# k^T v in three bursts instead of five, in a linear-attention and GeGLU block on Trainium2

## The chip, the core and the metric

One core of one Trainium2 chip runs the kernel. The metric is the device time of one execution in microseconds (us). A core has five engines that run side by side, each through its own instructions in order: TensorE (PE, matmuls; its weight loads are listed as PEld), VectorE (DVE), ScalarE (ACT), GpSimd (Pool) and SyncE (SP, which issues the DMAs). They wait for one another through semaphores. A DMA is issued on an engine's queue and lands later.

## The reference, cut to what matters

One sequence of 2048 rows of 640 numbers goes through attention with a feature map instead of a softmax over positions, and then through a GeGLU feed-forward net (1536 wide). There are 32 heads of 20. Shortened:

```python
q, k, v = split(layernorm(x) @ wqkv)             # 32 heads of 20 each
phi_q = [softmax(q @ w_phi), softmax(-(q @ w_phi))]
phi_k = [softmax(k @ w_phi), softmax(-(k @ w_phi))]
kv  = sum over rows of phi_k^T v                 # per head, 40 x 20
z   = sum over rows of phi_k
o   = (phi_q @ kv) / (phi_q . z + 1e-6)
h   = x + o @ wo
out = h + (gelu(layernorm(h) @ w_gate) * (layernorm(h) @ w_up)) @ w_down
```

## The kernel before, in words

**Tiles.** The 2048 rows are 16 tiles of 128. A first stage (up to about 67 us) makes k and v of every tile, and out of them `kv`, the sum over all rows; from then on attention and feed-forward run tile by tile, woven together. The change is in the first stage.

**Weights folded first.** `w_phi` is multiplied into the weights of k and q: `fold` (line 232) makes `Wk2` from the transposed `WkT`, one 128-row piece `d` at a time, into a PSUM tile `wa`, which ACT empties where `d` is in `KA` (line 48, `QA` for q) and DVE elsewhere (lines 256 to 259). The five pieces of k are folded between lines 471 and 482; the five of q at the tiles in `FQ` (line 50), from pieces of `WqT` that `load_T` (line 200) issues on SP as transposing DMAs at the tiles in `LQ` (line 49).

**One tile of the first stage.** The main loop (line 494) does for each tile t: the layer norm of tile t+6 (`ln_ap`, on ACT), which goes to `LN1T` by a transposing DMA on SP; `k_tile` (line 331): ten 128x320 matmuls into `pk` and two exponentials on ACT into `E` (plus and minus); `v_mm` and `v_ev` (lines 301, 315) for tile t+3: ten matmuls into `pv`, evicted by ACT to `vS`, one of `NV` buffers (line 71); and `k_norm` (line 343): DVE sums E over each head (line 347) and takes the reciprocal `rs` (line 351), and two products divide E by it (line 355). Pool does the product of the minus half always and that of the plus half for the tiles in `VP` (line 47); for the others DVE does the plus half, put off into the next tile's `k_norm` (lines 348 and 364), for the last tile at once (line 361).

**k^T v.** `kv_tile` (line 368) adds one tile to `kvp`: 32 matmuls with 32 columns of weights and 40 columns of data each, one per head, four of them side by side in PE's array. They need the tile's two products and its `vS`. The order is written out by hand: `KVG` (line 56) says after which tile's k matmuls which tiles are added (after 6: 0 and 1; after 9: 2 to 4; after 13: 5 to 8); `KVQ` (line 57) puts tiles 9 to 12 behind the first group of q matmuls, and line 539 adds 13 to 15 at the end. Such a run of k^T v matmuls is called a burst. `kv_mask` (line 377) then takes `kvp` through DVE to `KV`, which the first `attn_a` needs.

**q.** `q_mm` (line 387) makes q of one or two column blocks (`QG`, line 52) for 512 rows, 5 or 10 matmuls of 128x512 into `pq`, and `q_exp` (line 399) exponentiates on ACT. Four groups, `QT` (line 53), are done at t=15: groups 0, 1 and 2 of ten matmuls and group 3 of five; the others after `kv_mask` (lines 831 on).

**What sets the order.** Engines follow the program's order. PSUM tiles of this stage (`gtile`, line 111) share four buffers: a tile waits until the one that held its buffer before has been emptied. `kvp` is one of them (line 496).

Of the kernel before, what the change touches and what calls it, by code (L numbers as in the profile page):

```python
# [17 lines left out]
def kernel(  # L18
# [19 lines left out]
    NT = S // P  # L38
    NB = NT // 4
    NC = D // P  # L40
# [3 lines left out]

    H0 = [(P * c) // Dh for c in range(NC)]
    NH = [(P * c + P - 1) // Dh - H0[c] + 1 for c in range(NC)]
    VP = (0, 2, 4, 6, 7, 9, 11, 12)
    KA, QA = (0, 1, 4), (0, 1, 2, 3, 4)
    LQ = (7, 9, 9, 9, 10)
    FQ = (10, 11, 12, 13, 14)  # L50

    QG = ((5, 6), (0, 1), (2, 3), (4,), (7, 8), (9, 10), (11, 12), (13, 14), (15,), (16,), (17,), (18,), (19,))
    QT = (15, 15, 15, 15)
    T3 = 3

    KVG = {6: (0, 1), 9: (2, 3, 4), 13: (5, 6, 7, 8)}
    KVQ = {0: (9, 10, 11, 12)}
    VC = Dh + 1
    KC = Dh + 2

# [7 lines left out]
    SLOT = [(5 * (c // 2) + 2 * (c % 2), 3 * (c // 2) + c % 2, 2 + c % 2) for c in range(NC)]  # L68
    SL = 12
    DC = 512 - 9 * KC  # L70
    NV = 11

    x_v = A_x.rearrange("b (p t) d -> p (b t) d", t=NT)
    o_v = out.rearrange("b (p t) d -> p (b t) d", t=NT)
# [36 lines left out]
    def gtile(name):  # L111
        return psG.tile([P, 2, 512], F32, name=name, tag="G")
# [65 lines left out]

    vF = [p1.tile([P, H * VC + 11], BF16, name=f"vS{i}") for i in range(NV)]
    vS = [v[:, 0:H * VC].rearrange("p (h f) -> p h f", f=VC) for v in vF]  # L180
# [30 lines left out]
    ones = nc.const_aps.tensor(1.0, [P, 512], BF16)  # L211
    for i in range(NV):
        nc.vector.memset(vS[i][:, :, 0], 1.0)
    make_identity(nc, ident)
    nc.gpsimd.memset(hmask, 1.0)
    for c in range(NC):
# [4 lines left out]
                                compare_op=ALU.is_ge, fill=0.0, base=Dh - 1 - off, channel_multiplier=-1)  # L221
    for i in range(NV):
        nc.gpsimd.memset(vF[i][:, H * VC:], 1.0)
# [8 lines left out]
    def fold(WT, W2, quarters, ds=range(NC)):  # L232


        n, w = (2, QF) if quarters else (1, HD)
        runs = []
        for c in range(NC):
            lo, hi = H0[c] * Dh, (H0[c] + NH[c]) * Dh
            for r in range(2 * n):
                a, b = max(lo, r * w), min(hi, (r + 1) * w)  # L240
                if a < b:
                    runs.append((r // n, r, c, a, b))
        runs.sort()
        for d in ds:
            wa = gtile("wa")
            wr = wa.rearrange("p u (q x) -> p (u q) x", q=n)
            for i, (u, r, c, a, b) in enumerate(runs):
                nc.tensor.matmul(wr[:, r, a - r * w:b - r * w], lhsT=WT[:, c, d * P:(d + 1) * P],  # L248
                                 rhs=BD[:, c].rearrange("p a b -> p (a b)")[:, a - H0[c] * Dh:b - H0[c] * Dh],
                                 start=(i == 0 or runs[i - 1][0] != u),  # L250
                                 stop=(i + 1 == len(runs) or runs[i + 1][0] != u), skip_group_check=True)
            dst, src = W2[:, d, :].rearrange("p (u f) -> p u f", u=2), wr[:, :, 0:w]
            if quarters:
                dst = W2[:, d, :].rearrange("p (c r f) -> p r c f", c=NC, r=4)
                src = src.rearrange("p r (c f) -> p r c f", c=NC)
            if d in (QA if quarters else KA):
                nc.scalar.copy(dst, src)
            else:
                nc.vector.tensor_copy(dst, src)
# [19 lines left out]
    def ln_ap(t, on_act=False, on_pe=False):  # L279
        ln = (ln_act if on_act else ln_dve)(p1, "1", *lnp[t])  # L280
        if on_pe:
            lnp[t] = ln
        else:
            transpose_to(LN1T[t // 4][:, :, t % 4 * P:(t % 4 + 1) * P], ln, False)

    def ln_tp(t, on_dve=False):
        transpose_to(LN1T[t // 4][:, :, t % 4 * P:(t % 4 + 1) * P], lnp[t], True, on_dve)
# [13 lines left out]
    def v_mm(t, us=(0, 1)):  # L301
        if 0 in us:
            pv[t] = gtile("pv")
        proj(pv[t], t, Wv, us)
# [10 lines left out]
    def v_ev(t):  # L315
        nc.scalar.activation(vS[t % NV][:, :, 1:VC].rearrange("p (u h) f -> p u h f", u=2),
                             pv[t][:, :, 0:HD].rearrange("p u (h f) -> p u h f", f=Dh), ACTF.Copy,
                             scale=lnp[t][2] if t in CT else 1.0)
# [12 lines left out]
    def k_tile(t):  # L331
        if t in pks:
            pk = pks[t]
            k_part(t, NC - 1)
        else:
            pk = gtile("pk")
            proj(pk, t, Wk2)
        Ek[t] = ev.tile([P, 2, D], BF16, name="E", bufs=10)
        for s in range(2):
            nc.scalar.activation(Ek[t][:, s, :].rearrange("p (u f) -> p u f", u=2), pk[:, :, 0:HD],  # L340
                                 ACTF.Exp, scale=((lnp[t][2], nrstd[t]) if t in CT else (1.0, -1.0))[s])

    def k_norm(t):
# [9 lines left out]
        def mult(s, eng):  # L353
            e = Ek[t][:, s, :].rearrange("p (h f) -> p h f", f=Dh)
            eng.tensor_tensor(e, e, rs[:, s * H:(s + 1) * H, None].to_broadcast([P, H, Dh]), ALU.mult)  # L355

        mult(1, nc.gpsimd)
        if t in VP:
            mult(0, nc.gpsimd)
# [8 lines left out]
    def kv_tile(t):  # L368

        E = Ek[t].rearrange("p s (h f) -> p s h f", f=Dh)  # L370
        for i in range(QH):
            for r in range(4):
                h = r * QH + i
                nc.tensor.matmul(kvp[QUAD[r], :, i * Dh:(i + 1) * Dh], lhsT=vF[t % NV][:, h * VC:h * VC + 32],  # L374
                                 rhs=E[:, :, h, :], start=(i == t == 0), stop=(t == NT - 1), skip_group_check=True)

    def kv_mask():

        for s in range(2):
            dst = bass.AP(KT[s].tensor, KT[s].offset, [KT[s].ap[0], [Dh + 32, QH], [1, Dh]])  # L380
            nc.vector.tensor_scalar(dst, kvp[:, s].rearrange("p (h f) -> p h f", f=Dh), sc[:, s:s + 1], bi[:, s:s + 1],
                                    op0=ALU.mult, op1=ALU.add)
            nc.vector.transpose(KV[s].rearrange("p n j -> p (n j)"), KT[s])
# [3 lines left out]
    def q_mm(j, part=(0, 1), kcs=range(NC)):  # L387

        if 0 in part and 0 in kcs:
            pqs[j] = gtile("pq")  # L390
        for i, bc in enumerate(QG[j]):
            if i not in part:
                continue
            b, c = divmod(bc, NC)
            for kc in kcs:
                nc.tensor.matmul(pqs[j][:, i, :], lhsT=Wq2[:, kc, c * P:(c + 1) * P], rhs=LN1T[b][:, kc, :],  # L396
                                 start=(kc == 0), stop=(kc == NC - 1))

    def q_exp(j, signs=(0, 1)):
        for s in signs:  # L400
            nc.scalar.activation(Eq[j][:, :, s, :], pqs[j][:, 0:len(QG[j])], ACTF.Exp, scale=(1.0, -1.0)[s])  # L401
# [66 lines left out]
    ln_st(4, act=False, between=lambda: ln_ap(3, on_pe=True))  # L468
    ln_tp(3, True)
    nc.sync.dma_start(x_sb[1][:, 2:4, :], x_v[:, 6:8, :])  # L470
    fold(WkT, Wk2, False, (0,))
    v_ev(2)
    fold(WkT, Wk2, False, (1,))
    ln_st(5, act=False, between=lambda: ln_ap(4))
    nc.sync.dma_start(x_sb[2][:, 0:2, :], x_v[:, 8:10, :])
# [18 lines left out]
    for t in range(NT):  # L494
        if t == T3:
            kvp = gtile("kvp")[:, 0, 0:2 * QF].rearrange("p (s f) -> p s f", s=2)
        late = t in (1, 4)
        if 0 < t < NT - 6 and not late:
            ln_ap(t + 6, on_act=True)
        k_tile(t)  # L500
        if t == 0:
            ln_ap(6)
            nc.sync.dma_start(x_sb[3][:, 0:2, :], x_v[:, 12:14, :])
        if t in FQ:
            fold(WqT, Wq2, True, [i for i, f in enumerate(FQ) if f == t])
        for i in KVG.get(t, ()):
            kv_tile(i)
        for j in range(len(QT)):
            if t == QT[j]:
                q_mm(j)  # L510
                q_exp(j)
                for i in KVQ.get(j, ()):
                    kv_tile(i)
        if 0 < t < NT - 3:
            v_mm(t + 3)
        if late:
            ln_ap(t + 6, on_act=True)
        if t == 1:
            nc.sync.dma_start(x_sb[3][:, 2:4, :], x_v[:, 14:16, :])
        if 0 < t < NT - 3:  # L520
            v_ev(t + 3)
        for i in ST.get(t, ()):
            ln_st(i, i + 1)
        k_norm(t)
        load_T(WqT, 0, *[i for i, f in enumerate(LQ) if f == t])
        if t == 10:
            transpose_to(LN1T[0][:, :, P:2 * P], ln_a(1), False)
        if t == 13:
            ln_ap(0, on_act=True)
        if t == 8:  # L530
            for z in KT:
                nc.gpsimd.memset(z, 0.0)
        if t == 13:
            nc.sync.dma_start(Wo, wo_v)
    q = len(QT)
    nc.gpsimd.tensor_copy(Wg[:, 0, 0:1], Eq[q - 2][:, 0, 1, 0:1])
    for a, b in ((0, 2), (2, 4)):
        nc.sync.dma_start(Wg[:, a:b], wg_v[:, a:b])
    for t in range(13, NT):
        kv_tile(t)  # L540
    kv_mask()
    ev_cm.__exit__(None, None, None)
    p1_cm.__exit__(None, None, None)
# [393 lines left out]
```

## Time and profile before

| | us |
|---|---|
| median of three runs | 272.1 (272.08 to 272.21) |
| the profiled execution | 272.0 |
| its span on the core | 270.3 |
| bursts of k^T v, first to last matmul start | 30.7 to 67.0 |
| first matmul of attn_a(0) | 69.1 |

The profile's page comes from one execution. Its views used here: the busy time of each engine; the chain of work that ended last, which is followed back from the last instruction to what released each step; the waits, which say for an idle engine what ended the idle time; and the timeline, where a row has start, length, engine, line, operation, output<-inputs, shapes and count, and in brackets the idle time before it and what ended it. Rows of one kind that follow each other are merged. Starts of matmuls are measured and their ends modelled, so that a difference of starts is the better measure. The granted TensorE clock is 1.00 in every stretch from 15 us on.

### The profile page before, as it was taken

Reading aid. Unit: us, or ns where it says so; the run is one execution under the profiler, and the core shown is the slowest. Engines: PE = TensorE matmul, PEld = TensorE weight load, DVE = VectorE, ACT = ScalarE, POOL = GpSimd, SP = SyncE. Lnnn points to the kernel's source line nnn. Section 1 sums busy time; section 2 is a strip of 40 time slices with the busy share of each in tenths; the row PEclk is TensorE's granted clock in tenths of the full one; section 3 lists DMA queues with packets and bytes.
Section 4 is the critical chain, followed back from the end, with each engine's and each line's share of the span. In section 5 each row is a group of like instructions: output and inputs, shape, how many; then the busy total and the mean of one; then the engine's idle time right before and its main releaser. Section 6 shows DMA issues by size and latency. Waiting matters only on the chain.

```text
span 270.3 us, 7032 instructions
## 1 busy us (share of the span) xinstructions
PE 265.5 (98%) x2851; PEld 171.7 (64%) x2867; DVE 176.4 (65%) x348; ACT 138.1 (51%) x248; POOL 99.5 (37%) x236
## 2 busy tenths in 40 slices
PE   8999999999999999999999999999999999999995
PEld 6777777764455887788755455775555476444574
DVE  5899999998876758876566783568663322333322
ACT  5769997887789675245541356321544300322100
POOL 5448988794002335376211664014561100000000
PEclk9999999999999999999999999999999999999999
DMA  7998255240678432332201224103222101000011
GB/s 192 213 203 175 54 86 100 62 127 26 233 260 232 155 101 62 41 98 51 52 24 51 49 50 51 49 2 78 78 41 52 24 24 51 24 0 0 4 49 49
DMA packets 45264, 22.10 MB, mean 82 GB/s; under 512 B 37808, under 2 KB 43184, under 8 KB 45232
## 3 DMA queue, kind: packets, MB, share of 16 engines
q1 hardware_dynamic: 44576, 21.64, 33.0%
q8 instruction: 22, 0.36, 0.6%
q10 hardware_dynamic: 656, 0.03, 0.2%
q14 instruction: 10, 0.08, 0.1%
HBM read 10.18 MB, written 2.62 MB: 47 GB/s over the span
## 4 chain that ended last, share of the span: by engine, by line
PE 87%; SPq 4%; DVE 2%; POOL 2%; DMA 2%; issue 1%; ACT 1%; ACTq 0%; POOLq 0%
PE gu L767 38%; PE pd L789 20%; PE po L707 8%; PE pq L396 8%; PE pk L296 5%; PE pv L296 4%; SPq L203 2%; PE kvp L374 2%; DMA x_sb<-in_A_x_dram 2%; PE ab L618 1%; POOL E L355 1%; DVE stats L121 1%; PE ab L585 1%; PE wa L248 1%; DVE sk L347 1%
## 5 line engine op out<-in xcount | busy, mean ns | idle before, releaser
L770 ACT ACTIVATE g<-gu 128x512 bf16<-128x512 f32 (+1 forms) x60 | 30.4, 510 | 74.0 <-PE gu L767 73.2
L773 DVE TENSOR_TENSOR GT<-gu,g 128x512 bf16<-128x512 f32 (+1 forms) x60 | 34.4, 580 | 46.6 <-PE gu L767 38.8
L767 PE MATMUL gu<-LN2T,Wg 128*128 128x512 bf16 (+1 forms) x290 | 61.3, 335 | 0.5
L767 PE MATMUL gu<-LN2T,Wu 128*128 128x512 bf16 (+1 forms) x300 | 61.8, 336 | 0.0
L789 PE MATMUL pd<-Wd,GT 128*128 128x320 bf16 (+4 forms) x396 | 53.9, 295 | 0.0
L789 PEld LDWEIGHTS <-GT 128*128 128x128 bf16 x396 | 37.6, 98 | 14.5 <-DVE GT L773 0.2
L767 PEld LDWEIGHTS <-Wu 128*128 128x128 bf16 x300 | 29.4, 98 | 22.6
L767 PEld LDWEIGHTS <-Wg 128*128 128x128 bf16 x300 | 29.0, 98 | 21.2
L296 PEld LDWEIGHTS <-LN1T 128*128 128x128 bf16 x290 | 28.0, 98 | 10.6 <-issue 0.2
L355 POOL TENSOR_TENSOR E<-E,rs 128x640 bf16<-128x640 bf16 x24 | 30.2, 1288 | 6.5 <-DVE rs L351 6.2
L791 DVE TENSOR_TENSOR y<-pd,x_sb 128x320 bf16<-128x320 f32 (+4 forms) x33 | 15.8, 480 | 24.1 <-PE pd L789 24.1
L707 PE MATMUL po<-Wo,oT 128*128 128x320 bf16 x160 | 24.5, 299 | 0.0
L296 PE MATMUL pk<-Wk,LN1T 128*128 128x320 bf16 x160 | 24.4, 299 | 0.0
L396 PE MATMUL pq<-LN1T,Wq 128*128 128x512 bf16 x94 | 22.6, 379 | 0.3
L347 DVE TENSOR_REDUCE sk<-E 128x64 f32<-128x1280 bf16 x16 | 22.9, 1430 | 0.0
L401 ACT ACTIVATE Eq<-pq 128x1024 bf16<-128x1024 f32 (+1 forms) x26 | 19.9, 832 | 2.9 <-PE pq L396 2.7
L707 PEld LDWEIGHTS <-oT 128*128 128x128 bf16 x160 | 15.6, 98 | 7.3 <-ACT oT L165 0.2
L340 ACT ACTIVATE E<-pk 128x640 bf16<-128x640 f32 x28 | 18.7, 746 | 2.7 <-PE pk L296 2.7
L296 PE MATMUL pv<-Wv,LN1T 128*128 128x320 bf16 x130 | 19.8, 299 | 0.1
L151 ACT ACTIVATE ln<-x_sb,v,rstd 128x640 bf16<-128x640 bf16 x14 | 12.9, 920 | 13.0 <-POOL v L746 12.8
L396 PEld LDWEIGHTS <-Wq 128*128 128x128 bf16 x100 | 9.4, 98 | 10.3
L682 DVE TENSOR_TENSOR tt<-AB,w 128x1280 bf16<-128x1280 f32 x10 | 15.1, 1506 | 0.4 <-POOL w L675 0.3
(120 smaller groups left out, 292.3 us busy)
## 6 DMA issues: line engine op xcount, KB each, us to landing
out_dram<-y SPq DMA_DIRECT2D x15, 160.0 KB, 1.8
x_sb<-in_A_x_dram SPq DMA_DIRECT2D x6, 320.0 KB, 3.9
Wu<-in_B_w_up_dram SPq DMA_DIRECT2D x1, 1920.0 KB, 8.8
Wg<-in_B_w_gate_dram SPq DMA_DIRECT2D x2, 768.0 KB, 6.6
Wd<-in_B_w_down_dram SPq DMA_DIRECT2D x1, 1440.0 KB
Wo<-in_A_wo_dram SPq DMA_DIRECT2D x1, 800.0 KB, 5.5
x_sb<-in_A_x_dram SPq DMA_DIRECT2D x4, 160.0 KB, 3.3
Wv<-in_A_wqkv_dram SPq DMA_DIRECT2D x2, 320.0 KB, 4.2
```

Of the source, the lines that this page charges most:

```text
L296: nc.tensor.matmul(ps[:, u, 0:HD], lhsT=lnT(t, c), rhs=W[:, c, u * HD:(u + 1) * HD], start=(c == 0), stop=(c == NC - 1))
L340: nc.scalar.activation(Ek[t][:, s, :].rearrange("p (u f) -> p u f", u=2), pk[:, :, 0:HD], ACTF.Exp, scale=((lnp[t][2], nrstd[t]) if t in C ...
L347: nc.vector.reduce_sum(sk, Ek[t].rearrange("p s (h f) -> p (s h) f", f=Dh), axis=AX.X)
L355: eng.tensor_tensor(e, e, rs[:, s * H:(s + 1) * H, None].to_broadcast([P, H, Dh]), ALU.mult)
L396: nc.tensor.matmul(pqs[j][:, i, :], lhsT=Wq2[:, kc, c * P:(c + 1) * P], rhs=LN1T[b][:, kc, :], start=(kc == 0), stop=(kc == NC - 1))
L401: nc.scalar.activation(Eq[j][:, :, s, :], pqs[j][:, 0:len(QG[j])], ACTF.Exp, scale=(1.0, -1.0)[s])
L707: nc.tensor.matmul(pos[u], lhsT=st[t][:, c, :], rhs=Wo[:, c, u * HD:(u + 1) * HD], start=(c == 0), stop=(c == NC - 1))
L767: nc.tensor.matmul(gu[i][:, 0:n], lhsT=W[:, c, f * P:(f + 1) * P], rhs=LN2T[b][:, c, a0:a1], start=(c == 0), stop=(c == NC - 1))
L770: nc.scalar.activation(g[:, 0:n], gu[0][:, 0:n], ACTF.Gelu_apprx_tanh)
L773: nc.vector.tensor_tensor(st[b, "g", f][:, a0:a1], gu[1][:, 0:n], g[:, 0:n], ALU.mult)
L789: nc.tensor.matmul(pd[:, 0:f1 - f0], lhsT=st[b, "g", f][:, tl * P:(tl + 1) * P], rhs=Wd[:, f, f0:f1], start=(f == 0), stop=(f == NF - 1), ...
L791: nc.vector.tensor_tensor(y[:, f0:f1], pd[:, 0:f1 - f0], x_sb[b][:, tl, f0:f1], ALU.add)
```

## The change

- `KVG` and `KVQ`: k^T v is done in three bursts: tiles 0 to 3 after tile 9's k matmuls, 4 to 8 after tile 13's, and 9 to 15 at the end. The bursts after tile 6 and behind the first q group are gone.
- `NV` is 12 instead of 11: one more buffer of `vS`, with its two memsets.
- The fourth q group (`pq(3)`, five matmuls) is split: two before the last burst, and three, with its exponentials, after it.
- Tile 13 joins `VP`: Pool does both of its products, DVE none.
- `KA` gets piece 3: ACT evicts it and DVE no longer does. `v_ev(2)` comes before fold 0 and not after it.
- `LQ`: W_q's second piece is transposed at tile 8 instead of 9, and so ahead of tile 15's own transpose on SP.

```diff
-    VP = (0, 2, 4, 6, 7, 9, 11, 12)
-    KA, QA = (0, 1, 4), (0, 1, 2, 3, 4)
-    LQ = (7, 9, 9, 9, 10)
+    VP = (0, 2, 4, 6, 7, 9, 11, 12, 13)
+    KA, QA = (0, 1, 3, 4), (0, 1, 2, 3, 4)
+    LQ = (7, 8, 9, 9, 10)
...
-    KVG = {6: (0, 1), 9: (2, 3, 4), 13: (5, 6, 7, 8)}
-    KVQ = {0: (9, 10, 11, 12)}
+    KVG = {9: (0, 1, 2, 3), 13: (4, 5, 6, 7, 8)}
...
-    NV = 11
+    NV = 12
...
+    v_ev(2)
     fold(WkT, Wk2, False, (0,))
-    v_ev(2)
     fold(WkT, Wk2, False, (1,))
...
             if t == QT[j]:
-                q_mm(j)
-                q_exp(j)
-                for i in KVQ.get(j, ()):
-                    kv_tile(i)
+                q_mm(j, kcs=range(2 if j == len(QT) - 1 else NC))
+                if j < len(QT) - 1:
+                    q_exp(j)
...
-    for t in range(13, NT):
+    for t in range(9, NT):
         kv_tile(t)
+    q_mm(q - 1, kcs=range(2, NC))
+    q_exp(q - 1)
     kv_mask()
```

## The prediction

> **What bounds the kernel now.** I read the page's first section, the chain of work that ended last in order of time, and the timeline by engine round each burst of k^T v.
>
> ```profile
> PE 265.5 (98%) x2851; PEld 171.7 (64%) x2867; DVE 176.4 (65%) x348; ACT 138.1 (51%) x248; POOL 99.5 (37%) x236
> ```
>
> TensorE (PE) has work 98% of the time. The chain says from where on that is also what ends last:
>
> ```profile
> 30.84 0.60 ACT E L340
> 31.44 0.04 issue
> 31.48 1.52 PE pv L296 x10
> ...
> 39.79 1.04 PE kvp L374 x96
> ...
> 53.14 1.17 PE kvp L374 x128
> ...
> 59.63 1.16 PE kvp L374 x123
> ...
> 66.29 0.87 PE kvp L374 x96
> ```
>
> Up to 31.44 us the chain runs through the x load at 11.48, VectorE's (DVE's) statistics and ScalarE (ACT); from 31.48 to the last output it is PE, so a microsecond taken out of PE's row there is one off the end, unless something PE waits for is no earlier. A burst is priced by starts, in the timeline:
>
> ```profile
> 29.29 1.52 PE L296 MATMUL pk<-Wk,LN1T 128*128 128x320 bf16 x10
> 30.75 0.68 PE L374 MATMUL kvp<-E,vS 128*32 128x40 bf16 x64
> 31.48 1.52 PE L296 MATMUL pv<-Wv,LN1T 128*128 128x320 bf16 x10
> ```
>
> Ten 128x320 matmuls take 1.36 from start to start, so without its burst pv(9) could begin at 30.65 and not 31.48: 0.83. The same sum gives 1.13 (t=9, 3 tiles), 1.26 (t=13, 4), 1.25 (t=15, 4) and 0.98 (last, 3). Matmuls in a burst start 8.3 ns apart (128: 1.24 less one matmul's 0.187, over 127), 0.264 a tile, and what remains is 0.20 a burst, whatever its size, for the turn from full tiles to 32-column tiles and back. Two bursts cost more than that line: t=6 by 0.10 (pv(9) needs ACT's E(5), which ends at 31.43) and t=9 by 0.14.
>
> **The change, part by part** (times of the trace before).
>
> *Folds.* PE stands before pv(3) because its PSUM buffer is the one ACT empties of fold 0:
>
> ```profile
> 11.62 0.69 ACT L257 CAST Wk<-wa 128x640 bf16<-128x640 f32 x1 [0.66 <-PE wa L248]
> 12.37 1.18 PEld L296 LDWEIGHTS <-LN1T 128*128 128x128 bf16 x9 [0.17 <-issue]
> ```
>
> v_ev(2) now goes first, into ACT's 0.66 of idle time (pv(2) is done at 10.99). By the built program's waits pv(3) then takes the buffer of tile 3's transpose, empty at 11.80: pv(3) at 12.11 for 12.37, 0.25. Of this 0.15 stays: pk(4) (23.86) needs E(2), which ends at 23.67, and ACT there hangs on ln(8) at 21.57, released by Pool's mr behind the x load. Fold 3's eviction, 0.69, fits into ACT's 1.01 idle before 15.64; without that hole it would delay E(0) by 0.69. DVE gets 0.82 free at 14.24 and spends it waiting for the x load until 15.60: nothing. One more pair of memsets (0.14 on DVE, 0.05 on Pool) lies in their idle time before 3.30 and 5.39.
>
> *Burst at t=6 gone*: -0.83. What is late next is ACT, some 2 us behind PE here. In the built program kvp takes its PSUM buffer at its first write, so it now takes it at t=9, and pv(9) waits for v_ev(7) (29.43) and not E(5). Checked one by one up to t=9, PE has 0.4 to 1.0 to spare on each buffer and LN1T landing (nearest: pk(7) at 31.85 against E(5) 31.43).
>
> *t=9 with 4 tiles*: 1.26 for 1.13, +0.13. *t=13 with 5*: +0.26. PE reaches pq(0) at 57.31-0.15-0.83+0.13+0.26 = 56.72.
>
> *W_q's second piece at t=8*: fold 1 of W_q would be 0.85 earlier, at 45.6, and the piece landed at 45.28; now it lands earlier. SP puts one issue, 1.3 to 2.1, ahead of tile 15's transpose (issue 40.61, landed 44.70, so about 45.6); pv(15) needs it at 49. The three pieces behind it keep their places. Cost 0; were that slack gone, up to 0.9.
>
> *Tail.* The t=15 burst goes; 32 of 35 pq matmuls (0.2157 each) now come before the last burst, which has 7 tiles: 56.72+6.90+0.09 = 63.71 for tile 9, and tile 15, six tiles on, at 65.30. LN1T's rewritten first block, which pq(1) reads at 58.9, is issued about 0.85 earlier than now (55.56) and lands about 57.8, by the 3.1 that such a transpose takes in the DMA section. So who is late for tile 15?
>
> ```profile
> 59.31 1.27 POOL L355 TENSOR_TENSOR E<-E,rs 128x640 bf16<-128x640 bf16 x1
> 59.50 1.77 DVE L355 TENSOR_TENSOR E<-E,rs 128x640 bf16<-128x640 bf16 x1
> 61.90 1.27 POOL L355 TENSOR_TENSOR E<-E,rs 128x640 bf16<-128x640 bf16 x1 [1.31 <-DVE rs L351]
> 63.65 0.76 DVE L355 TENSOR_TENSOR E<-E,rs 128x640 bf16<-128x640 bf16 x1
> 63.90 1.63 POOL L355 TENSOR_TENSOR E<-E,rs 128x640 bf16<-128x640 bf16 x1 [0.73 <-DVE rs L351]
> 64.33 1.89 DVE L355 TENSOR_TENSOR E<-E,rs 128x640 bf16<-128x640 bf16 x1
> 66.22 0.84 PEld L374 LDWEIGHTS <-vS 128*32 128x32 bf16 x96 [0.42 <-DVE E L355]
> ```
>
> DVE's product takes 0.8 alone; next to one of Pool's it ends 0.68 after Pool's end (61.27 after 60.58, 66.21 after 65.53; also at 39.59 and 46.61), and Pool's is 1.63 where DVE was first: the two exclude each other. Taking tile 13's 1.77 from DVE brings its chain forward: rs(14) 59.68, sum(15) 60.15, rs(15) 61.68, product 14 at 62.15. Pool, busy without a hole (1.227 start to start), does 13 twice to 61.80, 14 to 63.04. Then either DVE goes first (63.72), Pool's 15 ends at 64.84 and DVE's 15 at 65.53, or Pool goes first (64.27) and DVE does both by 65.60. Tile 15 starts at about 65.62, 0.32 after PE could. Before it started at 66.73 (66.22 and two tiles). Three more pq matmuls (0.65) now follow, so attn_a(0) moves by 1.11-0.65 = **0.46**. Its KV, done at 69.24 now, 2.27 after the last k^T v matmul began, is done at about 68.1, before the 68.68 at which attn_a(0) starts. Behind it every wait is fed by PE, and the chain there is PE: 1:1. That tile 13's second product is on Pool costs PE nothing else (ready 61.80, needed 64.77).
>
> [...]
>
> **Sum.** Profiled execution 272.0 (span 270.3 and 1.7 around it); it stands 0.1 below the median 272.1. 272.0-0.46 = 271.54, and on the median 271.65. Bounds of what is not shown: the hand-over, E(15) 65.5 to 65.6; gaps in long bursts, 0 to 0.14 per 96 matmuls (t=9's row, the only one with such a gap); I take 0, as three of four comparable rows have next to none.
>
> **Rivals.**
> - *Tile 15 is in time* (DVE's chain ends before 65.3): PE alone sets the tail, 66.73-65.30-0.65 = 0.78, 271.3. For it: PE has no other wait. Against: four rows of exclusion.
> - *Long bursts gap as at t=9*: +0.19, +0.23 and +0.28 ahead of tile 15, which starts at 66.0; gain 0.1, 272.0.
> - *kvp still holds a buffer from tile 3*, so the change does not free PE at t=6: pv(9) waits for E(5) at 31.43, PE is 0.99 later, 0.2 slower, 272.3. Against: the built program's waits.
> - *Slower: Pool, now without a hole from 54.40 on, makes E(15) later.* It decides from 66.08 (66.73-0.65) on. If Pool's 13, 14 and 15 each stretch or DVE loses each hand-over so that E(15) is as late as now (66.21), the three pq matmuls behind it make it 0.2 slower, 272.3; one more product waited for (1.27) makes 273.5. For it: DVE's and Pool's rows there are 89% and 54% busy and every contended product lengthened; against: the chain above ends 0.5 earlier in both orders.
>
> **How the numbers follow.** Forecast 0.47 (271.45 to 271.85), in time 0.20, gaps 0.10, buffer 0.06, Pool late 0.17. A measurement here can tell 0.2% (0.54) from no change. Faster by more, below 271.56: the second case and about a quarter of the first, 0.33. Slower by more, above 272.64 (E(15) after 66.6): 0.13 of Pool late's 0.17. Within: 0.54. Range 271.1 to 272.6: below it a few per cent, above it that 0.13.
>
> **What would show it.** pv(3) at 12.1; pk(4) at 23.7; pv(9) near 30.5 without a wait; pv(12) near 39.9; pk(14) near 53.65; a gap of about 0.3 inside the last burst before its last tile, released by DVE's E; attn_a(0) at 68.7. Wrong if that gap is missing (then 0.8), if it is over 0.8 (then slower), if pv(9) waits for ACT, or if PE stands after 69 where it did not.

## The result and the profile after

The changed kernel takes 275.36 us (median of 6 runs, 274.85 to 275.74) and the kernel before 272.15 in the same comparison: ratio 1.0109, 95% interval 1.0095 to 1.0123. It is 3.2 us slower, outside the range of the prediction. The profiled execution takes 275.48 us, with a span of 273.8 on the core, 3.5 more than before; the granted clock is 1.00 throughout.

PE's share on the page falls from 98% to 97%, with 1.0 us more of busy time:

```profile
PE 266.5 (97%) x2867; PEld 172.1 (63%) x2867; DVE 175.0 (64%) x347; ACT 139.0 (51%) x249; POOL 101.2 (37%) x238
```

The waits of PE over the whole span (us in total, times, the longest) name three that are new; the kernel before has only the 0.8 us at the very start in this list. The smallest is the 0.3 us that pk(4) waits for ACT's E; the other two are:

```profile
PE pq L395 <- issue: 1.9, 1, 1.9
PE pd L789 <- DVE GT L773: 1.3, 1, 1.3
```

The chain that ended last, in order of time, answers to the lines shown of before. The burst at t=6 is gone and nothing waits there; the bursts at t=9 and t=13 have 1.33 and 1.57 us in it; and behind the last stand 1.91 us of "issue", time in which PE waited for nothing that the profile shows:

```profile
64.44 1.93 PE kvp L373 x224
66.38 0.32 PE pq L395
66.70 1.91 issue
68.61 2.55 PE pq L395 x11
```

PE's timeline there. One of the 12 last Q matmuls runs, then PE stands; the next starts 2.30 us after it instead of 0.216, so 2.08 are lost:

```profile
66.31 0.39 PE L395 MATMUL pq<-LN1T,Wq 128*128 128x512 bf16 x1
68.61 2.55 PE L395 MATMUL pq<-LN1T,Wq 128*128 128x512 bf16 x11 [1.91 <-issue]
```

The second place is the first matmul of `down`. In the kernel before, it ran at 103.31 while the last two gate/up products (GT, 104.01 to 104.76) were still to come, and PE waited 0.15 for them behind the first 11 weight loads:

```profile
103.31 2.63 PE L789 MATMUL pd<-Wd,GT 128*128 128x326 bf16 x18
```

In the changed kernel one weight load runs at 105.15, and the first matmul only at 106.76, when the last product (the second of this row, to 106.71) has ended:

```profile
105.96 0.75 DVE L773 TENSOR_TENSOR GT<-gu,g 128x256 bf16<-128x256 f32 x2
106.76 2.62 PE L789 MATMUL pd<-Wd,GT 128*128 128x326 bf16 x18 [1.33 <-DVE GT L773]
```

So the time came in two lumps, told here from starts: attn_a(0) at 71.09 for 69.14, +1.95; the first result of `down` (y) at 108.61 for 105.18, +3.43, 1.48 of it new; and the end at +3.5. By stretch:

| us | before | predicted | after |
|---|---|---|---|
| pk(4) | 23.86 | 23.71 | 24.06 |
| pk(4) to pq(0) | 33.45 | 33.01 | 33.31 |
| pq(0) to attn_a(0) | 11.83 | 11.96 | 13.72 |
| attn_a(0) to the first y | 36.04 | 36.04 | 37.52 |

The four differences to the prediction, 0.35, 0.30, 1.76 and 1.48, make 3.89 of the 3.94 between the forecast for the profiled execution (271.54) and 275.48.

### The profile page after: what moved, and what is told of

It is laid out like the page before. It is cut to its first block, busy times and chain, and to the rows that moved or that the text cites. A ratio compares the mean times of both kernels' runs of the same rounds, so it can differ in the third digit from the quotient of the medians.

```text
span 273.8 us, 7046 instructions
## 1 busy us (share of the span) xinstructions
PE 266.5 (97%) x2867; PEld 172.1 (63%) x2867; DVE 175.0 (64%) x347; ACT 139.0 (51%) x249; POOL 101.2 (37%) x238
## 4 chain that ended last, share of the span: by engine, by line
PE 88%; DVE 3%; DMA 2%; issue 2%; POOL 2%; ACT 1%; SPq 0%; ACTq 0%
PE gu L767 37%; PE pd L789 19%; PE pq L395 8%; PE po L707 8%; PE pk L295 6%; PE pv L295 5%; DMA x_sb<-in_A_x_dram 2%; PE kvp L373 2%; PE ab L618 1%; PE ab L585 1%; DVE stats L120 1%; PE wa L247 1%; DVE tt L682 1%; PE tp L163 0%; POOL rstd L139 0%
## 5 line engine op out<-in xcount | busy, mean ns | idle before, releaser
L354 POOL TENSOR_TENSOR E<-E,rs 128x640 bf16<-128x640 bf16 x25 | 31.6, 1297 | 4.4 <-DVE rs L350 4.1
```

## The experiments

Two theories. **Instruction supply** (the stand at 66.5): PE's program is brought in while it runs, in packets from 12.69 to 258.03 us in the changed kernel's DMA records. Part 3 of the page has a queue for it (packets, MB, share of 16 engines):

```profile
q8 instruction: 22, 0.36, 0.5%
```

That is 16 KB a packet; the page counts 2867 matmuls and as many weight loads, 5734 instructions, or 260.6 for each of the 22; I took 256 a block, which is the distance between the two stands of `twice` below. A k^T v matmul and its weight load pass every 8.3 ns, so 256 instructions last 1.06 us in a burst. If the next block takes longer than that from its request to its use, a run stands that goes from one border of two blocks (named here by the number of the instruction behind it) to the next. The packet in question runs from 65.91 to 67.15 us in the trace's DMA records. Its rival: an operand or a buffer is late behind the burst. **PSUM turn** (the stand at 105): the four two-bank PSUM tiles of the first stage are handed out in an order that the change has shifted, so the banks of the first `down` matmul are now those that the last gate/up pair used; in the built program it waits for that pair's product. Its rival: this stand is an echo of the first one, or the folds' new order costs time itself.

### fold_back: the folds in the old order

```diff
-    v_ev(2)
     fold(WkT, Wk2, False, (0,))
+    v_ev(2)
     fold(WkT, Wk2, False, (1,))
```

> The changed kernel with one line moved back: V's eviction of tile 2 again behind the first fold, as before. Median of the changed kernel 275.36 us. Theory PSUM turn: the other order of the first folds turned the order in which the two-bank PSUM tiles are handed out, so that the first matmul of `down` lies in the bank that the last gate/up pair used, and waits for that pair's product on VectorE (PE stands 1.33 us at 105.4 in the changed kernel, x_sb's y comes 1.40 us later than the shift before it); with the order of before its bank is an older one, and the gap goes: 275.36 - 1.40 = 274.0 us, within 0.3. Rival A, follow-up: the gap at 105 us is only the echo of the stand at 66.5 to 68.6 us, which stays here: 275.4. Rival B, the x load (landed 18.46 instead of 17.49 us) is what the order of the folds costs: pk(4) 24.06 to 23.86, 275.2.

Measured: 274.36 (273.39 to 275.37, 6 runs), ratio to before 1.0061 [1.0032, 1.0090], 0.48% or 1.3 us less than the changed kernel's 1.0109. The stand at `down` is gone and the one at the Q matmuls is there, so it is no echo:

```profile
68.30 4.24 PE L395 MATMUL pq<-LN1T,Wq 128*128 128x512 bf16 x11 [2.23 <-issue]
```

The 11 Q matmuls behind the stand take 4.24 us here and 2.55 in the changed kernel. The table of stretches gives the reason (stretch, length, busy time and count of PE, PEld, DVE, ACT and POOL, granted clock, DMA share, GB/s): the clock went down to 0.50 behind the stand.

```profile
70.00:72.00 2.00, 2.00 (x6) 0.68 (x5) 0.00 (x0) 0.03 (x1) 0.00 (x0) 0.50 0.77 306
72.00:74.00 2.00, 1.84 (x47) 0.92 (x47) 0.88 (x1) 0.95 (x2) 0.00 (x0) 0.94 0.00 0
```

That costs this execution 1.7 us more. It is the only one of its six with a mean granted clock below 0.999 (0.994; in warm_p40 it is three of four, in b_tail one of six): a stand of this size has a second price, which only some executions pay.

### turn_1: the PSUM order turned, nothing moved

```diff
-    warm(*[512] * 2, *[P] * 28)
+    warm(*[512] * 2, *[P] * 27)
+    wu = gtile("wu")
+    warm(P)
```

> The changed kernel with the last of its 30 warm-up matmuls writing a PSUM tile of its own instead of the one that the others write: no instruction more, none in another place; only the order in which the four two-bank PSUM tiles are handed out is one place further from there on. Theory PSUM turn: the first matmul of `down` then lies in the banks of an older gate/up pair (the third last, as in the kernel before) and PE no longer stands 1.33 us for the last product: 275.36 - 1.40 = 274.0, within 0.5; the stand at the 12 last Q matmuls stays (2.1 to 2.3 us). Rival, the first folds' order itself costs time: 275.4, as the folds stay where they are.

Measured: 274.49 (274.18 to 274.99, 4 runs), 1.0068 [1.0046, 1.0090]. The first `down` matmul waits for nothing, and the folds are where the change has put them:

```profile
105.69 2.62 PE L791 MATMUL pd<-Wd,GT 128*128 128x326 bf16 x18
```

In ratio that is 0.41% or 1.1 us less than the changed kernel. The stand at the Q matmuls is there, in this execution 0.7 us longer (from the burst's start to the next Q matmul 4.94 us for 4.24; the packet came at 66.49 to 67.41). Releasers are inferred: the profile puts that stand down to DVE's KV (2.93), which is what happened to end just ahead of it.

### b_fold: the folds' new order alone, in the kernel before

The edit is the inverse of fold_back's, made in the kernel before.

> The kernel before with V's eviction of tile 2 ahead of the first fold, and nothing else. If the order of the first folds itself costs time, 1 us or more is seen here; PSUM turn: in this program the first `down` matmul waits for x_sb's add, ahead of the last product, so there is no stand at 103 us and the time stays within 0.4 us of before.

Measured: 273.44 (272.50 to 274.77, 10 runs), 1.0023 [1.0001, 1.0045], 0.6 over before, which is more than the 0.4 that I had allowed; no stand at `down` (104.29, without a wait). The profile has a stand elsewhere, for the other theory's reason: in the burst behind the first Q group the 119th matmul starts 0.41 us late, at the border 1723.

```profile
60.17 1.12 PE L374 MATMUL kvp<-E,vS 128*32 128x40 bf16 x118
61.52 0.25 PE L374 MATMUL kvp<-E,vS 128*32 128x40 bf16 x10 [0.23 <-issue]
```

The order of the folds itself costs at most a part of what fold_back and turn_1 took away: turn_1 keeps the new order, and its wait at `down` is gone. What is paid for at `down` is where the turn ends up, and that depends on everything allocated before it.

### warm_m24 and warm_p40: the same columns of warm-up in fewer or more instructions

```diff
-    warm(*[512] * 2, *[P] * 28)
+    warm(*[512] * 6, *[P] * 12)               # warm_m24: 18 matmuls
+    warm(*[512] * 2, *[P] * 8, *[64] * 40)    # warm_p40: 50 matmuls
```

> The changed kernel with the warm-up before the first tile written as 18 matmuls over the same 4608 columns instead of 30: 24 instructions fewer (a weight load and a matmul each) ahead of everything else on PE, nothing else changed. Theory instruction supply: PE's program comes in blocks of 16 KB, 256 instructions; in the changed kernel PE stands from 66.4 to 68.6 us because the block that begins at its instruction 1979 (the second of the 12 last Q matmuls) has not arrived; it was asked for when PE came past 1723, at about 65.2 us. With 24 instructions fewer in front the same border lies 24 instructions further on, at the first attention matmul, which PE reaches 11 x 0.216 = 2.4 us later: the stand falls from 2.09 us to 0 to 0.3, attn_a(0) 71.09 to 69.0 to 69.3, and the time to 275.36 - 1.9 = 273.5 us, within 0.3; the gap at 105 us stays. Rival A, operands or a buffer (tile 15's divide, Q's PSUM tile): nothing of that changes, PE stands after the same Q matmul for the same 2.1 us, 275.4. Rival B, follow-up: the gap at 105 us goes with the stand: 272.1.

> The changed kernel with the warm-up written as 50 matmuls over the same 4608 columns instead of 30: 40 instructions more on PE ahead of everything else. Theory instruction supply: the border at instruction 1979 now lies 40 instructions earlier in the work, 25 instructions into tile 15 of k^T v, that is after 12 or 13 of its 32 matmuls; PE stands there, in the middle of a run of matmuls that wait for nothing, for 2.0 to 2.3 us, and not at the Q matmul; k^T v ends so much later and attn_a(0) follows KV instead: 70.4 to 71.1 us end of chain, the time 275.2 to 276.4 us. Rival A, operands or a buffer: the stand stays between the first and the second of the last 12 Q matmuls, 275.4. Rival B, any run of 224 matmuls leaves PE standing at its end: the stand stays behind the last k^T v matmul, 275.4.

Measured, warm_m24: 273.74 (273.10 to 273.96, 5 runs), 1.0038 [1.0020, 1.0057]. No stand; 11.63 us from pq(0) to attn_a(0), 0.20 less than before; the wait at `down` is as long as it was:

```profile
64.10 2.00 PE L373 MATMUL kvp<-E,vS 128*32 128x40 bf16 x224
66.26 2.54 PE L395 MATMUL pq<-LN1T,Wq 128*128 128x512 bf16 x11 [0.16 <-issue]
```

warm_p40: 278.52 (277.83 to 279.46, 4 runs), 1.0224 [1.0198, 1.0251]. The stand has moved into the run, behind 6 tiles and 13 matmuls (205 = 192 + 13), where nothing is waited for. A second one, which I had not expected, is at 57.03, ahead of the W_q fold of t=14, where the border 1467 now lies:

```profile
57.03 0.49 PE L247 MATMUL wa<-BD,WqT 128*128 128x140 bf16 x8 [0.86 <-PE pk L295]
...
65.72 1.84 PE L373 MATMUL kvp<-E,vS 128*32 128x40 bf16 x205
69.85 0.30 PE L373 MATMUL kvp<-E,vS 128*32 128x40 bf16 x19 [2.28 <-issue]
```

24 instructions fewer take the stand away and 40 more move it by 40 instructions, with the operands, waits and transfers the same: it belongs to a place in PE's program and not to a piece of work. Most of warm_p40's excess over the expectation (2.1 to 3.3 us on the median) is that second stand, about 1.0 us from start to start, and the clock, down to 0.50 behind the other one: 4.22 us for 11 Q matmuls in the profiled execution.

### twice: two borders in one run

```diff
-    for t in range(9, NT):
+    for t in (*range(9, NT), *range(9, NT)):
         kv_tile(t)
```

> The changed kernel with the tail's seven tiles of k^T v issued twice in a row (they are added into k^T v twice, so the attention is another one): 896 small instructions in one run instead of 448. Instruction supply: the run passes two borders, 1979 and 2235. PE stands about 2.3 us at the first (after 224.5 of 448 matmuls), asks for the next block only when it comes past it, and stands about 2.3 us again at the second (after 352 or 353 matmuls): a block of 256 instructions per 3.4 us. attn_a(0) 71.09 + 1.9 (the 448 instructions) + 2.3 = 75.3, the time 279.6. Rival, a stand of its own that comes once, or that belongs to the Q matmuls behind the run: no stand within the run, one behind it, the time 275.4 + 1.9 = 277.3.

Measured: 283.85, one run. Both stands are within the run, 128 matmuls and their loads (256 instructions) apart:

```profile
63.99 2.01 PE L373 MATMUL kvp<-E,vS 128*32 128x40 bf16 x225
68.21 1.23 PE L373 MATMUL kvp<-E,vS 128*32 128x40 bf16 x128 [2.21 <-issue]
73.86 0.98 PE L373 MATMUL kvp<-E,vS 128*32 128x40 bf16 x95 [4.42 <-issue]
```

The places are as expected and the second stand is twice as long as I had said: W_g's load (two DMAs of 768 KB) filled the DMA engines from about 67 to 71.4 us, and the second packet runs from 71.42 to 72.45. The clock is at 0.50 from 68.51 to 78.75, which stretches the Q matmuls to 4.31.

### b_tail: the new tail alone, in the kernel before

```diff
-    KVQ = {0: (9, 10, 11, 12)}
...
-                q_mm(j)
-                q_exp(j)
-                for i in KVQ.get(j, ()):
-                    kv_tile(i)
+                q_mm(j, kcs=range(2 if j == len(QT) - 1 else NC))
+                if j < len(QT) - 1:
+                    q_exp(j)
...
-    for t in range(13, NT):
+    for t in range(9, NT):
         kv_tile(t)
+    q_mm(q - 1, kcs=range(2, NC))
+    q_exp(q - 1)
```

> The kernel before with the new tail alone: tiles 9 to 15 of k^T v in one run of 448 instructions behind the first three Q matmuls of the second group... the bursts at t=6, 9 and 13, V's buffers, Pool's list, the folds and W_q's pieces as before. Instruction supply: the tail begins at the same instruction 1530 as in the changed kernel and the border at 1979 lies again at the second of the 12 last Q matmuls: PE stands 2.1 to 2.3 us there, attn_a(0) 1.7 to 2.1 later than before. PSUM turn: in this program too the first `down` matmul waits for the last gate/up product (read from the built program), 1.33 us. So 272.3 + 1.9 + 1.4 = 275.6, within 0.5. Rival, the stand needs the changed bursts, folds or Pool's third divide: 272.3 to 273.7.

Measured: 276.01 (275.40 to 277.82, 6 runs), 1.0110 [1.0085, 1.0135], the whole loss of the change. Both stands are there:

```profile
PE kvp L373 <- issue: 2.4, 1, 2.4
PE pd L789 <- DVE GT L773: 1.3, 1, 1.3
```

So neither the bursts at t=9 and t=13 nor Pool's third divide nor the folds are needed for them.

### b_p40: the border moved in the kernel before

The edit is warm_p40's, in the kernel before.

> The kernel before, in which PE never stood for its program, with 40 instructions more in the warm-up (50 matmuls over the same 4608 columns instead of 30) and no other edit. Instruction supply: the border at instruction 1467 then falls at the end of pk(14), right behind the t=13 burst; the block behind it is asked for when PE comes past 1211, 8 matmuls into that burst (53.2 us), and is usable about 3.5 us later (56.7), while PE is there at 55.6: it stands 0.9 to 1.3 us ahead of the wa matmuls of t=14, though no run of small matmuls in this kernel is longer than 256 instructions. Elsewhere no border comes sooner than 3.5 us after its request. So 272.5 + 1.1 = 273.6, between 273.2 and 274.0. Rival, only a run of more than 256 small instructions starves PE: no stand, 272.5.

Measured: 273.02 (272.15 to 273.59, 10 runs), 1.0008 [0.9994, 1.0022]: a miss. In the profile pk(14), just there, takes 1.79 us where it takes 1.53 else, so 0.26 are lost and not 0.9 to 1.3; its ninth matmul starts at 56.89, 1.26 behind the packet's end at 55.63. The packet began at 53.96, 0.46 before PE came past 1211 in this execution (54.42): a packet can begin some tens of instructions ahead of the border, not at it as I had counted. By the DMA records of before and of the changed kernel the ten packets from 112 us on do so too, with PE 35 to 53 instructions ahead of a border (counted on from 1979 in steps of 256).

### b_bursts, bursts_wo and b_wo: without the long tail

```diff
-    KVG = {6: (0, 1), 9: (2, 3, 4), 13: (5, 6, 7, 8)}
+    KVG = {9: (0, 1, 2, 3), 13: (4, 5, 6, 7, 8)}     # b_bursts, bursts_wo
-    NV = 11
+    NV = 12                                          # b_bursts, bursts_wo
-        if t == 13:
+        if t == 10:                                  # bursts_wo, b_wo
             nc.sync.dma_start(Wo, wo_v)
```

> The kernel before with the bursts alone: t=6 burst gone, four tiles at t=9, five at t=13, V in 12 buffers; the tail as before (9 to 12 behind the first Q group, 13 to 15 later). No run crosses a border early, and the first `down` matmul waits for an older event than the last product. From pk(4) to pq(0) 33.45 falls to about 33.3, as in the runs of the changed kernel (1.40 and 1.64 us for the two bursts instead of 0.75, 1.11 and 1.24, and a turn each of 0.20 less): 0.15 below before, ratio 0.9990 to 1.0005. As forecast in the prediction (0.44 below): 0.9984.

> The kernel before with the bursts alone, as in b_bursts, and the load of W_o issued at t=10 instead of t=13 (about 48 us instead of 56.8, into a stretch in which the DMA engines move almost nothing). In b_bursts PE stood 2.93 us after 119 of the 128 matmuls behind the first Q group, at its instruction 1723; the packet with the next block began at 61.67 us, just behind W_o's transfer (58.7 to 61.5 us), 4 us after PE had come past 1467. Theory, the block's packet waits behind bulk transfers on the same DMA engines: with these free the packet starts within about 1 us of the request and the block is usable 3 us after it, at 60.7, before PE is at 1723 (61.1): no stand, the spread of the runs (272.5 to 277.1 in b_bursts) shrinks to about 1 us, and the ratio to 0.9985 to 1.0005. Rival, the block's latency has nothing to do with the transfers: the stand stays in the profile, and the ratio at 1.004.

> The kernel before with W_o's load issued at t=10 instead of t=13, and nothing else: the control of the run above. In the profile of before the block's packet began at 57.88 us, just ahead of W_o's transfer, and PE never stood; in single runs it may have. So 0 to 0.4 below before, ratio 0.9985 to 1.0005, with fewer runs above 273.5. If the earlier load itself costs time (the transposes of LN1T at 51.7 us, the folds of W_q), it is seen here: over 1.001.

Measured: b_bursts 274.40 (272.51 to 277.14, 10 runs), 1.0043 [1.0015, 1.0070]; bursts_wo 273.04 (272.07 to 274.74, 11 runs), 1.0025 [1.0004, 1.0045]; b_wo 272.93 (272.14 to 274.16, 12 runs), 1.0018 [1.0002, 1.0034]. All three lie above what I had expected (1.0005 at most). The profiled execution of b_bursts is the slowest of its ten and is used only for where its time went. It stands in the four-tile burst behind the first Q group, at instruction 1723, 256 below the other place, in a run that has the same 256 instructions as in the kernel before:

```profile
59.98 1.13 PE L374 MATMUL kvp<-E,vS 128*32 128x40 bf16 x119
64.04 0.23 PE L374 MATMUL kvp<-E,vS 128*32 128x40 bf16 x9 [2.93 <-issue]
```

The share of the 16 DMA engines in slices of 0.175 us from 57 to 64 (in tenths) is, for b_bursts:

```profile
DMA  9993009613187889999999972130000000000000
```

W_o's load, issued at 56.84, keeps them busy up to 61.2 us; the packet with PE's block begins at 61.67. With W_o issued at 53.84 (it waited on SP behind a transpose, so it was not as early as I had meant), the engines are free from 59.1 on:

```profile
DMA  9999999999190000000000000000000003000000
```

The packet begins at 59.06, and PE stands 0.30 us at the same matmul:

```profile
61.56 0.23 PE L374 MATMUL kvp<-E,vS 128*32 128x40 bf16 x9 [0.30 <-issue]
```

In these profiles the packet starts when the bulk transfers end, 2.6 us sooner in the second. The times say less: the two intervals overlap, and b_wo, the control, is itself slower than before, with a stand of 0.51 at the same place. That the block's packet waits behind other transfers is what these two profiles and the one of twice show; how much of the spread between runs it explains stays open. The kernel before comes to the same place with nothing to spare: its packet runs from 57.88 to 59.21, and the 119th matmul starts at 60.54, 1.33 behind it and 0.05 after the one ahead of it, where the others follow in 0.008.

### back_m24, turn_m24, turn_m24_wo: both stands taken out

back_m24 has fold_back's and warm_m24's edits. turn_m24 undoes no line of the change; turn_m24_wo has W_o's load at t=10 as well.

```diff
-    warm(*[512] * 2, *[P] * 28)
+    warm(*[512] * 6, *[P] * 11)
+    wu = gtile("wu")
+    warm(P)
```

> Both of the two edits before together: the order of the first folds of before, and 24 instructions fewer in the warm-up. If the two losses are separate and the theories hold, both go: 275.36 - 1.40 - 1.9 = 272.1 us, and with the t=6 burst gone (0.83 less) against the longer bursts at t=9 and t=13 (0.15 and 0.13 more than I had) and the tail's 0.46, 271.5 to 272.3, about the kernel before (272.15). If one of the losses was the other's echo, one of the single edits already gives this time, and this adds nothing to it. If neither theory holds: 275.4.

> The changed kernel with both losses taken out by the warm-up alone: 18 matmuls over the same 4608 columns, the last into a PSUM tile of its own. No line of the change is undone. Theory: neither the stand at the Q matmuls nor the one at the first `down` matmul is there, and what is left of the change is its own work: from pk(4) to pq(0) 33.28 us as in the runs with 24 instructions fewer (before 33.45), from pq(0) to attn_a(0) 11.63 (before 11.83), so 0.2 + 0.15 = 0.35 below before, 272.0 if before is at 272.35 in these runs, between 271.6 and 272.4. Rival, a loss of the change that the two stands have hidden (Pool's third divide, the x load): 272.5 or more.

> The changed kernel with the warm-up in 18 matmuls, the last into a PSUM tile of its own (as in turn_m24: no stand at the Q matmuls, none at the first `down` matmul), and W_o's load issued at t=10. Theory: all three places in which PE could wait for its program or for a PSUM bank are cleared, and what the change saves of its own is left: 0.17 from pk(4) to pq(0) and 0.20 from pq(0) to attn_a(0), ratio 0.9975 to 0.9995 to the kernel before. Rival, turn_m24 had no such waits left and W_o's load is neutral: 0.9990 as there.

Measured: back_m24 272.24 (271.59 to 273.29, 10 runs), 1.0000 [0.9985, 1.0016]; turn_m24 272.44 (271.97 to 273.48, 12 runs; before 272.72), 0.9990 [0.9977, 1.0003]; turn_m24_wo 272.58 (12 runs; before 272.46), 1.0003 [0.9988, 1.0018]. With both stands gone the loss is gone, in turn_m24 by edits to the warm-up alone; what then remains of the change cannot be told from nothing, and the 0.9975 to 0.9995 expected of turn_m24_wo did not come. turn_m24's Q matmuls follow the burst (from 64.77) as closely as in warm_m24:

```profile
66.93 2.54 PE L397 MATMUL pq<-LN1T,Wq 128*128 128x512 bf16 x11 [0.16 <-issue]
```

### The stands side by side

The end of the block's packet in the DMA records against PE's next matmul start, in eleven kernels' profiles (times in us):

| kernel | packet | PE goes on | behind the packet's end |
|---|---|---|---|
| changed | 65.91 to 67.15 | 68.61 | 1.46 |
| fold_back | 65.62 to 66.70 | 68.30 | 1.60 |
| turn_1 | 66.49 to 67.41 | 69.06 | 1.65 |
| warm_p40, both | 54.54 to 55.50, 67.17 to 68.35 | 57.03, 69.85 | 1.53, 1.50 |
| b_tail | 68.03 to 68.90 | 70.24 | 1.34 |
| twice, both | 65.57 to 66.86, 71.42 to 72.45 | 68.21, 73.86 | 1.35, 1.41 |
| b_bursts | 61.67 to 62.64 | 64.04 | 1.39 |
| bursts_wo | 59.06 to 60.13 | 61.56 | 1.43 |
| b_wo | 59.01 to 60.09 | 61.44 | 1.35 |
| b_fold | 58.72 to 60.19 | 61.52 | 1.33 |
| b_p40 | 53.96 to 55.63 | 56.89 | 1.26 |

Each of these stands ends 1.26 to 1.65 us after its packet does, wherever the packet lies, and nowhere in the 16 profiles does PE start on a block sooner than 1.26 us behind its packet. With 0.9 to 1.7 us for the packet itself, a block needs 2.2 to 2.9 us from the packet's start in these stands, more than twice what a burst takes for 256 instructions.

## Why the prediction was wrong, point by point

- **"gaps in long bursts, 0 to 0.14 per 96 matmuls (t=9's row, the only one with such a gap); I take 0"** is the step that failed. I took a burst's rate, 8.3 ns a matmul, from runs of 64 to 128 matmuls and carried it to 224. Those rows could not show the limit: no run of theirs is longer than 256 instructions. A run of more than 256 instructions, 128 of these matmuls, can pass one border and come to the next before its block is there; here the price was 2.08 us in the profiled execution, where my upper bound for a gap in this run was 0.28. (A shorter run can stand as well, where the packet is late: b_bursts.) The page did show the queue (22 packets of instructions); I read past it because its share of the DMA engines is 0.5%. A packet is 16 KB, and the two stands of twice are 256 instructions apart: with the first one behind it, PE ran through those 256 in 1.23 us and stood again, for 4.42. In this run of matmuls of 8.3 ns the supply was not hidden.
- **"Behind it every wait is fed by PE, and the chain there is PE: 1:1"** failed at the first `down` matmul, 1.48 of the 3.94. I had followed the PSUM tiles of the first stage through the built program (pv(3), pv(9), kvp) and stopped there; the order goes on turning through the attention and into `down`'s first bank. The wait could be read in the built program before the run: in the changed kernel the first `down` matmul names the last product, in the kernel before an older one.
- **Folds**, pv(3) at 12.11: it came at 12.07. That pk(4) would gain 0.15 did not show: the x load landed at 18.46 instead of 17.49 and E(2) came later (pk(4) waited 0.34 for it). The term was smaller than the spread of what it rests on: pk(4) is at 23.71 to 24.96 in the 16 profiles, with the same code ahead of it in several.
- **Burst at t=6 gone**: right. pv(9) starts without a wait, 6.79 us after pk(4) for 7.62 before, 0.83 less.
- **Bursts at t=9 and t=13**: +0.30 and +0.40 instead of +0.13 and +0.26 (pv(9) to pv(12) 9.58 for 9.28; pv(12) to pk(14) 13.88 for 13.48), 0.17 and 0.14 more, where the rival with gaps had 0.19 and 0.23. Each has a gap of 0.11 to 0.13 near the start of its fourth tile; in the profile of before the burst of three tiles has one too, in its third tile, and that of t=13 has none. In the measure of the prediction (1.13 and 1.26 before) they take 1.43 and 1.66 here, and in the other profiles with these bursts 1.35 to 1.43 and 1.65 to 1.69, but for fold_back's 1.57 and 1.56. What makes the gap was not tried. With it, more than four fifths of what t=6 gave is used up: pk(4) to pq(0) is 33.31, and 33.24 to 33.34 in nine more profiles with these bursts, against 33.45 (before), 33.36 (b_fold) and 33.27 (b_wo) with the old ones; warm_p40, b_tail and b_p40 have further waits in this stretch.
- **Tail**: the 0.32 of waiting for E(15) did not come. DVE's last product ended at 65.88, as late as the two exclude each other (0.67 after Pool's last at 65.21, as the 0.68 of before), but PE began the run at 64.37 and not at 63.71, so tile 15's turn was at 65.96. Where the instruction supply was out of the way (warm_m24, turn_m24), pq(0) to attn_a(0) took 11.63, the figure of the rival "tile 15 is in time" (its 0.78 less the 0.59 that belonged to earlier steps), 0.20 less than before. "Pool late" is refuted: Pool was through at 65.21.
- **The rivals**: three of the four were about a tile or a buffer that comes late, and one about gaps as a price per matmul. None asked what PE itself needs besides operands: its program.

## What to carry to other kernels

Count the instructions of a run of small matmuls, and not only their time: here 256 of them pass in 1.06 us while the block behind them needs 2.2 us or more from its packet's start, and that start itself came later where bulk loads ran (61.67 us in b_bursts, 59.06 in bursts_wo), and 24 instructions fewer ahead decided whether PE came to the next border with its block still on the way (2.08 us lost in the changed kernel, no stand in warm_m24). When a change adds, drops or reorders PSUM tiles, look in the built program at what the first matmul of every later stage waits for, down to the last stage, since the order is handed on. And a loss of a few microseconds that "issue" stands for is told from a late operand by one cheap run: change the number of instructions ahead and see whether the stand stays with the work or with the count.

## What the runs showed of the hardware that I had not expected

- PE's program comes in 16 KB packets (22 of them), 256 instructions each by the distance of the two stands of twice, and PE stood for up to 4.42 us where a block was late. It went on 1.26 to 1.65 us after the packet's end in each of 13 stands.
- In three profiles the packet of a block began where a bulk load ended: at 61.67 us behind W_o's load, busy up to 61.2 (b_bursts), at 59.06 with that load issued 3.00 us earlier and the engines free from 59.1 on (bursts_wo), and at 71.42 behind W_g's, busy up to 71.4 (twice).
- The granted clock can fall behind a stand. By the traces' clock records it fell to 0.50 at 68.82 (fold_back), 70.37 (warm_p40), 64.96 (b_bursts) and 68.51 us (twice), behind stands of 2.23, 2.28, 2.93 and 2.21 us and 0.30 to 0.92 us after PE had gone on. It was down for 3.41 us each time, and in twice, where the second stand of 4.42 us lies in it, for 10.24. It stayed at 1.00 behind the stands of 1.91 (changed) and 2.35 us (b_tail). The trace of turn_1 has no clock records, but the 11 Q matmuls behind its 2.93 us took 2.54, as in the changed kernel (2.55) and not the 4.24 of fold_back. So the length of the stand alone does not say whether the clock falls; what else decides was not shown.
